# A length-48 first transform on the four quarters of the TensorE array, in a fused Fourier and mixture-of-experts kernel

## The chip, the cores and the metric

The kernel runs on one core of a Trainium2 chip. The metric is the device time of one execution in microseconds (us), as the median of the runs shown. A core has a matrix engine (TensorE, PE in the rows; PEld is its weight load), a vector engine (VectorE, DVE), an activation engine (ScalarE, ACT), a general engine (GpSimd, POOL) and a queue for transfers (SyncE, SP). Each works through its own instructions in order and waits for the others by semaphores.

## What is computed

```python
X = rfft(x, axis=1)                    # x: 8 batches, 3072 positions, 256 channels
Yr = Xr @ w_r - Xi @ w_i + b_r         # and Yi = Xr @ w_i + Xi @ w_r + b_i
Y = soft_threshold(Yr, 0.01) + 1j * soft_threshold(Yi, 0.01)
y = irfft(Y, n=3072, axis=1)           # 24576 tokens of 256 channels
logits = y @ phi                       # 32 slots of 8 experts
slot_out = experts(softmax(logits, 0).T @ y)      # relu(s @ w1[e]) @ w2[e]
z = softmax(logits, 1) @ slot_out
out = (silu(z @ w_gate) * (z @ w_val)) @ w_out
```

## The kernel before

The program has two parts. The first (`phase1`, up to about 584 us, then the experts up to 612 us) goes over the eight batches; the second (from 612 us, lines 1540 to 1590) is one long loop for the gated product and is not touched. `phase1` is a list of tasks, each with an engine and what it needs; a table of numbers, `ORDER`, written out in the file, gives the order in which all tasks of all engines are issued. Rings (`plan.ring`) say how many buffers each kind of tile has; a task that opens a buffer comes after the last user of the one that it replaces.

A batch goes through these stages:

- **Loads.** `load_x` (L571, on SP) brings 64 of the 256 channels of a batch: 96 partitions, each with 32 neighbouring positions of 64 channels. There are two such buffers (`xq`). Batch 0 has four own buffers (`load_first`, L557).
- **Stage A** (`stage_a`, matmul L586, transpose L591). The 3072 positions are 96 rows by 32. One matmul contracts the 96 rows with a table `fwd` of 128 columns (real and imaginary parts of two sets of 32 frequencies) for 32 x 16 = 512 columns of data, into one PSUM bank of the ring `ac`, which has two. VectorE turns the bank in 32 x 32 blocks into `chan`. There are 16 such pairs of matmul and transpose in a batch, four to a loaded tile. All of this is float32.
- **Stage C** (`stage_c`, L612) finishes the transform: for each of 24 columns `j` a matmul of `chan` (contraction over 128 rows) with the table `cm`, four to a bank of the same ring `ac`. ScalarE and VectorE take the bank apart into a rounded part and a rest (`xg`, L628 and L631) and a sum (`sf`, `sg`, L634 to L650).
- **Stage B** (`stage_b`, L700) multiplies by the weights `whl`, three fp32r matmuls of 512 columns at a time, into the ring `pb`; L752 to L771 apply bias and threshold; L797 projects on `phi` and 64 small transfers `yi` (L826) rearrange the result.
- **Logits, slots, combine** (L865 to L1241) form logits, the running softmax and the slot sums. Between them `narrow` (L1201 to L1246) converts weights through a buffer `cv`.

Several stages already use parts of the array. L797 and L1103 have weights of 32 columns and put four products into four groups of 32 output partitions; L1522 does it with two groups of 64. All of them contract over all the rows that they have from partition 0.

At the end of `phase1` the expert weights (16 transfers of 1 MB, L427 and L432, on POOL) go into buffers that stages A to C give up. `hold` (L1387) issues spare matmuls.

Of the kernel before, what the change touches and what calls it, by code (L numbers as in the profile page):

```python
# [10 lines left out]
F32 = mybir.dt.float32  # L11
# [12 lines left out]
R2 = 32  # L24
NCH = 24
# [7 lines left out]
def dft_tables():  # L33
# [7 lines left out]
    n1 = np.arange(R1)  # L41
    n2 = np.arange(R2)
    k2 = np.arange(R2)
    sign = np.where(k2 >= R2 // 2, -1.0, 1.0)
    alt1 = np.where(n1 % 2 == 0, 1.0, -1.0)
    alt2 = np.where(n2 % 2 == 0, 1.0, -1.0)
    k1 = np.array([[j, 23 + j] for j in range(NCH)])
    k1[0] = (0, 47)

    fwd = np.zeros((R1, 4, 32))  # L50
    mix = np.zeros((4, R2, NCH, 2, 2, R2))
    for j in range(NCH):
        for h in range(2):
            if j == 0 and h == 0:
                fwd[:, 0, 0] = 1.0
                fwd[:, 1, 0] = alt1
                for i in range(R2):
                    if i == 0:
                        mix[0, :, j, 0, h, 0] = 1.0
                        continue  # L60
                    src = 0 if i < 16 else 1
                    k = 96 * i if i < 16 else 48 + 96 * (i - 16)
                    a = 2 * np.pi * ((n2 * k) % n) / n
                    mix[src, :, j, 0, h, i] = np.cos(a)
                    mix[src, :, j, 1, h, i] = -np.sin(a)
                continue
            a = 2 * np.pi * ((n1 * k1[j, h]) % R1) / R1
            fwd[:, 2 * h, j] = np.cos(a)
            fwd[:, 2 * h + 1, j] = -np.sin(a)
            a = 2 * np.pi * ((n2[:, None] * (k1[j, h] + 96 * k2)[None, :]) % n) / n  # L70
            mix[2 * h, :, j, 0, h, :] = np.cos(a)
            mix[2 * h + 1, :, j, 0, h, :] = np.sin(a)
            mix[2 * h, :, j, 1, h, :] = -np.sin(a) * sign
            mix[2 * h + 1, :, j, 1, h, :] = np.cos(a) * sign
# [64 lines left out]

    small = np.concatenate(  # L140
        [
            pad(np.concatenate([np.zeros((R1, 8)), fwd.reshape(R1, 128)], 1), R1),
# [17 lines left out]
for _n, _w in (  # L160
# [11 lines left out]
FWD = 136  # L172
# [1523 lines left out]
```

## Time and profile before

| | |
|---|---|
| median of 3 runs | 1693.27 us (1691.08 to 1694.23) |
| the profiled execution, its own time | 1693.74 us |
| its span, first to last instruction | 1691.6 us |
| mean granted TensorE clock | 0.998 |
| PE busy | 1662.7 us, 98% |
| VectorE busy | 1296.0 us, 77% |
| ScalarE busy | 980.7 us, 58% |
| GpSimd busy | 312.5 us, 18% |

Busy time is the union of an engine's instructions. A line of a group gives the source line, the engine, the operation, output and inputs, shapes and count, then busy time, mean nanoseconds of one, the idle time of the engine before them and what ended it. A float32 matmul shows as two records of the same form, so a count of x4 is two matmuls; a fp32r one shows as one. The records of matmuls that follow each other overlap, so the mean of one record is longer than what it adds; the chain of waits shows what each adds.

### The profile page before, as it was taken

Reading aid. Unit: us, or ns where it says so; the run is one execution under the profiler, and the core shown is the slowest. Engines: PE = TensorE matmul, PEld = TensorE weight load, DVE = VectorE, ACT = ScalarE, POOL = GpSimd, SP = SyncE. Lnnn points to the kernel's source line nnn. Section 1 sums busy time; section 2 is a strip of 40 time slices with the busy share of each in tenths; the row PEclk is TensorE's granted clock in tenths of the full one; section 3 lists DMA queues with packets and bytes.
Section 4 is the critical chain, followed back from the end, with each engine's and each line's share of the span. In section 5 each row is a group of like instructions: output and inputs, shape, how many; then the busy total and the mean of one; then the engine's idle time right before and its main releaser. Section 6 shows DMA issues by size and latency. Waiting matters only on the chain.

```text
span 1691.6 us, 23302 instructions
## 1 busy us (share of the span) xinstructions
PE 1662.7 (98%) x8178; PEld 1284.8 (76%) x8178; DVE 1296.0 (77%) x2203; ACT 980.7 (58%) x1830; POOL 312.5 (18%) x360
## 2 busy tenths in 40 slices
PE   7999999999999889999999999999999999999998
PEld 4677776776777558888888888888888888888886
DVE  5788888888778458778777777777777777877776
ACT  2655664655657246666656655665666656655664
POOL 1234433334444521100200200200010110110000
PEclk9999999999999999999999999999999999999999
DMA  9465666766556981311311311311230131131111
GB/s 193 88 139 120 123 123 144 138 142 122 126 132 216 310 200 26 81 26 26 81 19 20 82 25 26 70 37 25 41 66 15 24 81 26 25 72 26 25 26 25
DMA packets 260036, 139.94 MB, mean 83 GB/s; under 512 B 210224, under 2 KB 243728, under 8 KB 259920
## 3 DMA queue, kind: packets, MB, share of 16 engines
q1 hardware_dynamic: 246592, 105.03, 31.0%
q0 software_dynamic: 12272, 33.17, 7.2%
q8 instruction: 65, 1.06, 0.3%
q10 hardware_dynamic: 1056, 0.26, 0.1%
q14 instruction: 51, 0.42, 0.1%
HBM read 72.74 MB, written 40.50 MB: 67 GB/s over the span
## 4 chain that ended last, share of the span: by engine, by line
PE 94%; DMA 3%; DVE 1%; POOL 1%; ACT 0%; issue 0%; SPq 0%; DVEq 0%; ACTq 0%
PE o L1572 47%; PE pb L700 11%; PE pg L1547 8%; PE pv L1548 8%; PE ac L586 7%; PE ac L612 5%; PE ch L797 1%; PE ch L865 1%; PE ch L1055 1%; DMA w1s<-in_moe_w_dram 1%; PE ch L1103 1%; DMA w2s<-in_moe_w_dram 1%; PE ch L925 1%; PE ch L1011 1%; PE po L1460 1%; DMA xq<-in_x_dram 0%
## 5 line engine op out<-in xcount | busy, mean ns | idle before, releaser
L1572 PE MATMUL o<-hh,wo 128*128 128x512 f32 x2304 | 722.5, 395 | 0.0
L1550 ACT ACTIVATE sg<-pg 128x512 f32<-128x512 f32 x576 | 344.6, 598 | 413.8 <-PE pg L1547 413.8
L1552 DVE TENSOR_TENSOR h<-sg,pv 128x512 f32<-128x512 f32 x576 | 393.2, 683 | 248.6 <-ACT sg L1550 245.3
L1572 PEld LDWEIGHTS o<-hh,wo 128*128 128x128 f32 x2304 | 434.2, 188 | 100.8
L1572 PE MATMUL o<-hl,wo 128*128 128x512 f32 x1152 | 453.8, 394 | 0.0
L1560 DVE TENSOR_TENSOR hl<-h,hh 128x512 fp32r<-128x512 f32 x576 | 396.7, 689 | 0.1
L1559 ACT ACTIVATE hh<-h 128x512 fp32r<-128x512 f32 x576 | 359.4, 624 | 0.3 <-DVE h L1552 0.2
L1572 PEld LDWEIGHTS o<-hl,wo 128*128 128x128 f32 x1152 | 216.1, 188 | 51.9
L1547 PE MATMUL pg<-cst,gstk 96*128 96x512 f32 x576 | 227.7, 395 | 0.0
L1548 PE MATMUL pv<-cst,gstk 96*128 96x512 f32 x576 | 226.1, 393 | 0.6 <-DVE gstk L1533 0.6
L700 PE MATMUL pb<-xg,whl 128*128 128x512 f32 x576 | 179.3, 441 | 0.0
L700 PEld LDWEIGHTS pb<-xg,whl 128*128 128x128 f32 x576 | 105.3, 189 | 46.5 <-issue 25.1
L1548 PEld LDWEIGHTS pv<-cst,gstk 96*128 96x128 f32 x576 | 109.7, 190 | 25.9 <-DVE gstk L1533 0.9
L1547 PEld LDWEIGHTS pg<-cst,gstk 96*128 96x128 f32 x576 | 108.1, 188 | 25.7 <-DVE gstk L1533 0.8
L771 POOL TENSOR_TENSOR yt<-r,yt 128x512 f32<-128x512 f32 x74 | 96.6, 1305 | 153.5 <-ACT yt L762 103.2
L591 DVE STREAM_TRANSPOSE chan<-ac 128x512 f32<-128x512 f32 x128 | 89.8, 708 | 34.1 <-PE ac L586 29.8
L1608 POOL TENSOR_TENSOR e<-e,rs 96x256 f32<-96x256 f32 x28 | 22.6, 834 | 498.8 <-DVE rs L1605 498.8
L586 PE MATMUL ac<-xq,fwd 96*128 96x512 f32 x224 | 110.3, 598 | 1.2 <-DVE chan L591 0.7
L612 PEld LDWEIGHTS ac<-cm,chan 128*128 128x128 f32 x768 | 101.0, 196 | 12.1 <-issue 4.5
L612 PE MATMUL ac<-cm,chan 128*128 128x128 f32 x768 | 105.3, 283 | 0.0
L700 PE MATMUL pb<-sg,whl 128*128 128x512 f32 x288 | 86.7, 425 | 0.0
L634 ACT ACTIVATE sf<-ac 128x256 f32<-128x256 f32 x96 | 36.5, 381 | 78.5 <-PE ac L612 74.4
(151 smaller groups left out, 1481.1 us busy)
## 6 DMA issues: line engine op xcount, KB each, us to landing
out_dram<-ob SPq DMA_DIRECT2D x190, 128.0 KB, 2.8
yi<-yt SPq DMA_DIRECT2D x368, 64.0 KB, 2.1
xq<-in_x_dram SPq DMA_DIRECT2D x28, 768.0 KB, 8.1
cst<-c_scr POOLq DMA_DIRECT2D x72, 128.0 KB, 3.1
w1s<-in_moe_w_dram POOLq DMA_DIRECT2D x8, 1024.0 KB, 9.0
w2s<-in_moe_w_dram POOLq DMA_DIRECT2D x8, 1024.0 KB, 10.9
x<-in_x_dram SPq DMA_DIRECT2D x4, 768.0 KB, 10.1
cv<-in_moe_w_gate_dram SPq DMA_DIRECT2D x6, 512.0 KB, 6.0
```

Source lines behind the costliest of these rows:

```text
L586: nc.tensor.matmul(out=pt, lhsT=fwd[:, 8 - 8 * dh:136 - 8 * dh], rhs=T[kq][:, :, d1:d1 + 16], start=True, stop=True)
L591: nc.vector.transpose(out=chan[:, 12 * dh:12 * dh + 16, d0:d0 + 16, :].rearrange("p j d i -> p d j i"), in_=T[ka].rearrange("p n d -> p d n"),
L612: nc.tensor.matmul(out=pt[:, :, q:q + 2, i // 2, :], lhsT=chan[:, 16 * dh + j // 2, :, j % 2], rhs=cm[:, j, :].rearrange("p (c h k) -> p c ...
L700: nc.tensor.matmul(out=pt, lhsT=w[:, dh, m, es], rhs=xx, start=m != 1 and dh == 0 and n == 0, stop=dh == 1 and n == 2, skip_group_check=True,)
L771: e.tensor_sub(out=part(), in0=quarters(T[kr]), in1=part())
L1547: nc.tensor.matmul(out=pg, lhsT=gstk[:, 0, f * 128:(f + 1) * 128], rhs=rhs, start=True, stop=True)
L1548: nc.tensor.matmul(out=pv, lhsT=gstk[:, 1, f * 128:(f + 1) * 128], rhs=rhs, start=True, stop=True)
L1550: nc.scalar.activation(out=sg, in_=pg, func=AF.Silu)
L1552: nc.vector.tensor_mul(out=h, in0=sg, in1=pv)
L1559: nc.scalar.activation(out=hh, in_=h, func=AF.Copy)
L1560: nc.vector.tensor_sub(out=hl, in0=h, in1=hh.bitcast(F32))
L1572: nc.tensor.matmul(out=po_t[0][k], lhsT=w[:, f % 4, k * 128:(k + 1) * 128], rhs=a, start=(f == 0 and m == 0), stop=(f == NF - 1 and m == 2 ...
```

## The change

Positions are now 48 rows by two halves by 32: position = 64 p + 32 h + n. A length-48 transform with the same 64 columns (32 frequencies, real and imaginary) is made of each half h, and stage C joins the halves. The table `fwd` has 72 columns rather than 136 and stands twice in its tile, from partition 0 and from partition 64. Stage C keeps its form and count; only the numbers in `cm` differ.

A loaded tile holds one half of the sequence: channels 0 to 63 of a 128-channel group on partitions 0 to 47 and channels 64 to 127 on partitions 64 to 111, brought by two transfers (`load_x`, `load_x2`). The ring `xq` has three buffers rather than two. For batches 1 to 7 one task issues four matmuls of 48 rows by 64 columns by 512, one for each quarter of the array, into both banks of `ac`; two transposes follow. For batch 0 one task issues two matmuls, on two diagonal quarters, into one bank, and the second half of its loads is issued by ScalarE. The order table is new; it also gives 16 small subtractions from VectorE to GpSimd and takes one back, and four more spare matmuls.

```diff
 ORDER = [
-    2, 1, 0, 3, 4, 5, 40, 30, 50, 312, 48, 49, 6, 8, 7, 9, 10, 12, 11, 13,
...
-            ("xq", 2), ("tt", 2), ("ac", 2), ("xg", 2), ("sf", 2), ("sg", 1), ("pb", 3), ("r", 1), ("yt", 2), ("yi", 4),
+            ("xq", 3), ("tt", 2), ("ac", 2), ("xg", 2), ("sf", 2), ("sg", 1), ("pb", 3), ("r", 1), ("yt", 2), ("yi", 4),
...
-        fwd = apool.tile([R1, FWD], F32, name="fwd")
+        fwd = apool.tile([64 + R0, FWD], F32, name="fwd")
...
+        def half_x(k, r):
+            _, b, dh, c = k
+            d0 = 128 * dh + 64 * r
+            nc.sync.dma_start(
+                out=T[k][64 * r:64 * r + R0],
+                in_=x[b, :, d0:d0 + 64].rearrange("(p h n) d -> h p n d", h=2, n=R2)[c],
+            )
...
+        def stage_a0(dq, dd, rank):
...
+                for r in range(2):
+                    rows = slice(64 * r, 64 * r + R0)
+                    nc.tensor.matmul(
+                        out=pt[64 * r:64 * r + 64], lhsT=fwd[rows, 8 - 8 * dh:72 - 8 * dh],
+                        rhs=T["x0", dq][rows, :, 16 * dd:16 * dd + 16], start=True, stop=True, skip_group_check=True,
+                    )
...
+        def stage_a(b, dh, dd, rank):
+            kq = [("xq", b, dh, c) for c in range(2)]
...
+            def mm():
+                pt = [bank(k, [128, R2, 16], "ac") for k in ka]
+                for r, c in ((0, 0), (1, 1), (0, 1), (1, 0)):
+                    rows = slice(64 * r, 64 * r + R0)
+                    nc.tensor.matmul(
+                        out=pt[r][64 * c:64 * c + 64], lhsT=fwd[rows, 8 - 8 * dh:72 - 8 * dh],
+                        rhs=T[kq[c]][rows, :, d1:d1 + 16], start=True, stop=True, skip_group_check=True,
+                    )
...
+            for r in range(2):
+                add("DVE", turn(r), r=[ka[r]], w=[(*kt, ps[r])])
```

The new lines carry new numbers: L643 is the matmul of the quarters, L651 its transpose, L615 and L621 those of batch 0, L589 the load, L765 is the old L700, L677 the old L612, L862 the old L797, L891 the old L826, L1266 the old L1201, L1306 the old L1241, L1076 the old L1011, L1040 the old L975.

TensorE's order in the first stage A after batch 0 (batch 1, channels 0 to 127), before:

```order
L586 MATMUL ac<-xq,fwd 128x512
L700 MATMUL pb<-sg,whl 128x512 x3
L700 MATMUL pb<-xg,whl 128x512 x6
L586 MATMUL ac<-xq,fwd 128x512 x2
L700 MATMUL pb<-xg,whl 128x512 x3
L586 MATMUL ac<-xq,fwd 128x512 x2
L700 MATMUL pb<-xg,whl 128x512 x3
L586 MATMUL ac<-xq,fwd 128x512
L700 MATMUL pb<-xg,whl 128x512 x3
L586 MATMUL ac<-xq,fwd 128x512 x2
```

and the same place now:

```order
L643 MATMUL ac<-xq,fwd 64x512 x4
L765 MATMUL pb<-sg,whl 128x512 x6
L643 MATMUL ac<-xq,fwd 64x512 x4
L765 MATMUL pb<-xg,whl 128x512 x6
L643 MATMUL ac<-xq,fwd 64x512 x4
L765 MATMUL pb<-xg,whl 128x512 x6
L643 MATMUL ac<-xq,fwd 64x512 x4
L862 MATMUL ch<-yt,phis 32x256 x4
```

Eight matmuls of the old kind have become four groups of four; between two groups there are mostly six matmuls of stage B where three stood between two pairs.

TensorE's order in batch 5, from the end of channels 0 to 127 to the start of channels 128 to 255, before (from the last two matmuls on the second of the batch's four tiles to the first on the third):

```order
L586 MATMUL ac<-xq,fwd 128x512
L700 MATMUL pb<-xg,whl 128x512 x3
L586 MATMUL ac<-xq,fwd 128x512
L700 MATMUL pb<-xg,whl 128x512 x3
L1011 MATMUL ch<-td,csm 128x512
L612 MATMUL ac<-cm,chan 128x2x2x32 x8
L1011 MATMUL ch<-td,csm 128x512
L700 MATMUL pb<-sg,whl 128x512 x3
L1055 MATMUL ch<-vpad,csm 128x192 x4
L1061 MATMUL ch<-vt,csm 32x16 x2
L700 MATMUL pb<-sg,whl 128x512 x3
L586 MATMUL ac<-xq,fwd 128x512
```

and now:

```order
L643 MATMUL ac<-xq,fwd 64x512 x4
L765 MATMUL pb<-xg,whl 128x512 x3
L1076 MATMUL ch<-td,csm 128x512
L677 MATMUL ac<-cm,chan 128x2x2x32 x8
L765 MATMUL pb<-sg,whl 128x512 x3
L1076 MATMUL ch<-td,csm 128x512
L862 MATMUL ch<-yt,phis 32x256 x8
L677 MATMUL ac<-cm,chan 128x2x2x32 x4
L765 MATMUL pb<-sg,whl 128x512 x6
L765 MATMUL pb<-xg,whl 128x512 x3
L765 MATMUL pb<-sg,whl 128x512 x3
L643 MATMUL ac<-xq,fwd 64x512 x4
```

The work between the last group on one pair of tiles and the first group on the next pair is what stands in this list; the second tile of the next pair takes a buffer of the first pair.

The loads of batch 5 on the SP queue, before (the first three of its four tiles):

```order
L571 DMA xq<-in_x_dram 96x32x64
L826 DMA yi<-yt 32x2x256 x16
L571 DMA xq<-in_x_dram 96x32x64
L826 DMA yi<-yt 32x2x256 x16
L1241 DMA w_scr_60<-cv 128x512
L1201 DMA cv<-in_moe_w_out_dram 128x2x512
L571 DMA xq<-in_x_dram 96x32x64
```

and now (both halves of the third tile, then those of the fourth):

```order
L589 DMA xq<-in_x_dram 48x32x64 x2
L1306 DMA w_scr_60<-cv 128x512
L589 DMA xq<-in_x_dram 48x32x64
L1266 DMA cv<-in_moe_w_val_dram 128x1024
L589 DMA xq<-in_x_dram 48x32x64
L891 DMA yi<-yt 32x2x256 x16
```

One transfer of 96 partitions has become two of 48, and a conversion load (L1266) stands between the two halves of the tile that waits for its buffer.

## Rows read from the trace of the kernel before

**Rows 1.** The page: busy time, its 40 slices, and the chain by engine and line.

```profile
PE 1662.7 (98%) x8178; PEld 1284.8 (76%) x8178; DVE 1296.0 (77%) x2203; ACT 980.7 (58%) x1830; POOL 312.5 (18%) x360
...
PEclk9999999999999999999999999999999999999999
...
PE o L1572 47%; PE pb L700 11%; PE pg L1547 8%; PE pv L1548 8%; PE ac L586 7%; PE ac L612 5%; PE ch L797 1%; PE ch L865 1%; PE ch L1055 1%; DMA w1s<-in_moe_w_dram 1%; PE ch L1103 1%; DMA w2s<-in_moe_w_dram 1%; PE ch L925 1%; PE ch L1011 1%; PE po L1460 1%; DMA xq<-in_x_dram 0%
```

**Rows 2.** Windows: stretch, length, busy us (instructions) by engine, clock, DMA share, GB/s.

```profile
0.00:26.00 26.00, 17.87 (x34) 6.36 (x35) 11.65 (x20) 1.28 (x1) 0.70 (x6) 1.00 1.18 195
...
50.00:550.00 500.00, 497.45 (x2904) 359.28 (x2903) 421.28 (x750) 294.97 (x587) 189.50 (x178) 1.00 0.63 136
...
584.00:612.00 28.00, 23.67 (x233) 10.21 (x232) 4.18 (x37) 5.60 (x10) 9.81 (x15) 0.94 1.09 332
```

**Rows 3.** Groups of instructions: the first transform and the work moved between engines.

```profile
L586 PE MATMUL ac<-xq,fwd 96*128 96x512 f32 x224 | 110.3, 598 | 1.2 <-DVE chan L591 0.7 <-DMA xq<-in_x_dram 0.4
L771 POOL TENSOR_TENSOR yt<-r,yt 128x512 f32<-128x512 f32 x74 | 96.6, 1305 | 153.5 <-ACT yt L762 103.2 <-ACT r L762 29.3 <-DMA xq<-in_x_dram 10.7
L650 POOL TENSOR_TENSOR sg<-sf,sg 128x256 fp32r<-128x256 f32 x74 | 55.6, 755 | 99.2 <-ACT sg L646 92.3 <-DMA yi<-yt 4.7 <-issue 1.1
L771 DVE TENSOR_TENSOR yt<-r,yt 128x512 f32<-128x512 f32 x22 | 15.0, 683 | 5.0 <-ACT r L762 2.6 <-ACT yt L762 2.2
L650 DVE TENSOR_TENSOR sg<-sf,sg 128x256 fp32r<-128x256 f32 x22 | 9.4, 429 | 1.8 <-ACT sg L646 1.2 <-issue 0.5
```

**Rows 4.** Chain of waits from 105 us: start, us it adds, what.

```profile
108.12 0.93 PE ac L612 x8
...
113.57 1.72 PE ac L586 x4
115.29 0.70 PE pb L700 x3
115.99 1.00 PE ch L797 x16
...
119.16 0.86 PE ch L1011 x2
```

**Rows 5.** Timeline of VectorE from 14.9 us: batch 0's transposes back to back.

```profile
16.92 1.57 DVE L591 STREAM_TRANSPOSE chan<-ac 128x512 f32<-128x512 f32 x2 [0.36 <-PE ac L586]
18.86 1.57 DVE L591 STREAM_TRANSPOSE chan<-ac 128x512 f32<-128x512 f32 x2 [0.36 <-PE ac L586]
...
24.67 0.72 DVE L591 STREAM_TRANSPOSE chan<-ac 128x512 f32<-128x512 f32 x1 [0.36 <-PE ac L586]
```

**Rows 6.** Line L571 on the SP queue: nanoseconds of an issue, then us to landing.

```profile
L571 SPq DMA_DIRECT2D xq<-in_x_dram x28: 569/604/3834, 22.3 to 482.5; - x28
...
DMA to landing us min/median/max: 6.7/8.1/11.6
```

**Rows 7.** DMA issues: transfers, KB each, median us from issue to landing.

```profile
cv<-in_moe_w_val_dram SPq DMA_DIRECT2D x6, 512.0 KB, 4.1
```

**Rows 8.** Timeline from 0 us: first instructions of TensorE, and ScalarE's first.

```profile
8.13 17.36 PE L586 MATMUL ac<-x,fwd 96*128 96x512 f32 x30 [8.13 <-DMA fwd<-in_csmall_dram]
...
26.69 0.38 ACT L634 ACTIVATE sf<-ac 128x256 f32<-128x256 f32 x1 [24.66 <-PE ac L612]
```

**Rows 9.** Waits of TensorE on transfers: who, for what, us in total, times, longest.

```profile
PE po L1460 <- DMA w2s<-in_moe_w_dram: 3.2, 1, 3.2
...
PE ch L1103 <- DMA w2s<-in_moe_w_dram: 1.1, 1, 1.1
```

More of the change, by code (lines that the diff above doesn't have):

```diff
@@ L24 @@
 R2 = 32
+R0 = 48
 NCH = 24
@@ L41, in dft_tables @@
     n1 = np.arange(R1)
+    m1 = np.arange(R0)
+    m2 = np.arange(2 * R2)
     n2 = np.arange(R2)
@@ L45, in dft_tables, with put_mix @@
     alt1 = np.where(n1 % 2 == 0, 1.0, -1.0)
+    alt0 = np.where(m1 % 2 == 0, 1.0, -1.0)
     alt2 = np.where(n2 % 2 == 0, 1.0, -1.0)
[L47 to L51, printed above, removed]
-    for j in range(NCH):
+    k1 = np.array([[j, 48 + j] for j in range(NCH)])
+    k1[0] = (0, 24)
+    fwd = np.zeros((R0, 2, 32))
+    mix = np.zeros((2, 2, R2, NCH, 2, 2, R2))
+    def put_mix(part, j, c, h, i, v):
+        mix[:, part, :, j, c, h, i] = v.reshape((2, R2) + v.shape[1:])
@@ L53, in dft_tables @@
+    every = slice(None)
+    for j in range(NCH):
+        if j == 0:
+            fwd[:, 0, 0] = 1.0
+            fwd[:, 1, 0] = alt0
+        else:
+            a = 2 * np.pi * ((m1 * j) % R0) / R0
+            fwd[:, 0, j] = np.cos(a)
+            fwd[:, 1, j] = -np.sin(a)
         for h in range(2):
             if j == 0 and h == 0:
[L55 to L61, printed above, removed]
+                put_mix(0, j, 0, h, 0, np.ones(2 * R2))
+                for i in range(1, R2):
@@ L69, in dft_tables @@
[L69 to L74, printed above, removed]
+            a = 2 * np.pi * ((m2[:, None] * (k1[j, h] + 96 * k2)[None, :]) % n) / n
+            if j == 0:
+                put_mix(1, j, 0, h, every, np.cos(a))
+                put_mix(1, j, 1, h, every, -np.sin(a) * sign)
+                continue
@@ L76, in dft_tables @@
+            put_mix(0, j, 0, h, every, np.cos(a))
+            put_mix(1, j, 0, h, every, np.sin(a))
+            put_mix(0, j, 1, h, every, -np.sin(a) * sign)
+            put_mix(1, j, 1, h, every, np.cos(a) * sign)
     kn = 2 * np.pi * (np.outer(k2, n2) % R2) / R2
@@ L131, in dft_tables @@
     last[0:32, 0] = alt2
+    last[64:96, 0] = alt2
     fold = np.tile(np.eye(32), (4, 4))
@@ L138, in pad @@
         return z
+    first = np.zeros((128, FWD))
+    for r in range(2):
+        first[64 * r:64 * r + R0, 8:] = fwd.reshape(R0, 64)
     small = np.concatenate(
         [
-            pad(np.concatenate([np.zeros((R1, 8)), fwd.reshape(R1, 128)], 1), R1),
+            first,
             pad(gf.reshape(R1, 128), R1),
@@ L171 @@
     _o += _w
-FWD = 136
+FWD = 72
 SMW = _o
@@ L508, in load_f @@
         def load_f():
-            nc.sync.dma_start(out=fwd, in_=csmall[0:R1, 0:FWD])
+            nc.sync.dma_start(out=fwd, in_=csmall[0:64 + R0, 0:FWD])
         def mix_w():
@@ L551, in phase1, with load_first @@
         add("DVE", setup_small, w=["small", "vpad", "M"])
-        def load_first(dq):
+        def load_first(dq, r):
             def go():
-                T["x0", dq] = t = early.tile([R1, R2, 64], F32, name=f"x0{dq}")
-                nc.sync.dma_start(
-                    out=t, in_=x[0, :, dq * 64:(dq + 1) * 64].rearrange("(p n) d -> p n d", n=R2)
+                if ("x0", dq) not in T:
+                    T["x0", dq] = early.tile([64 + R0, R2, 64], F32, name=f"x0{dq}")
+                (nc.sync, nc.scalar)[r].dma_start(
+                    out=T["x0", dq][64 * r:64 * r + R0],
+                    in_=x[0, :, 64 * dq:64 * dq + 64].rearrange("(p h n) d -> h p n d", h=2, n=R2)[r],
                 )
@@ L566, in free_early, with load_x, load_x2, go @@
             ypool = open_pool("ypool")
[L568 removed]
+        def half_x(k, r):
[5 more added lines that the diff above has]
+            )
+        def load_x(k):
             def go():
[L570 to L578 removed]
+                sb(xpool, k, [64 + R0, R2, 64], "xq", 3)
+                half_x(k, 0)
+            return go
+        def load_x2(k):
+            def go():
+                half_x(k, 1)
+            return go
+        def stage_a0(dq, dd, rank):
             dh, d0 = dq // 2, (dq % 2) * 64 + dd * 16
[L580 to L582 removed]
+            ka = ("ac", "a", 0, 4 * dq + dd)
             def mm():
                 pt = bank(ka, [128, R2, 16], "ac")
[L586 to L588 removed]
+                for r in range(2):
[4 more added lines that the diff above has]
+                    )
             def turn():
@@ L594, in turn, with go @@
                 )
-            add("PE", mm, r=["f", kq, kt], w=[ka], new=[("ac", ka)] + ([("tt", kt)] if p % 8 == 0 else []))
-            add("DVE", turn, r=[ka], w=[(*kt, p)])
+            kt = ("tt", 0, dh)
+            add(
+                "PE", mm, r=["f", kt] + [("x0", dq, r) for r in range(2)], w=[ka], new=[("ac", ka)] + ([("tt", kt)] if d0 == 0 else []),
+            )
+            add("DVE", turn, r=[ka], w=[(*kt, 4 * dq + dd)])
+        def stage_a(b, dh, dd, rank):
+            kq = [("xq", b, dh, c) for c in range(2)]
+            kt = ("tt", b, dh)
+            ps = [8 * dh + 4 * r + dd for r in range(2)]
+            ka = [("ac", "a", b, p) for p in ps]
+            d1 = dd * 16
+            def mm():
[5 more added lines that the diff above has]
+                        rhs=T[kq[c]][rows, :, d1:d1 + 16], start=True, stop=True, skip_group_check=True,
+                    )
+            def turn(r):
+                def go():
+                    d0 = 64 * r + d1
+                    nc.vector.transpose(
+                        out=chan[:, 12 * dh:12 * dh + 16, d0:d0 + 16, :].rearrange("p j d i -> p d j i"),
+                        in_=T[ka[r]].rearrange("p n d -> p d n"),
+                    )
+                return go
+            add(
+                "PE", mm, r=["f", kt] + [(*k, r) for k in kq for r in range(2)], w=ka, new=[("ac", k) for k in ka] + ([("tt", kt)] if dd == 0 else []),
+            )
+            for r in range(2):
+                add("DVE", turn(r), r=[ka[r]], w=[(*kt, ps[r])])
         def stage_c(b, g, hb, dh, rank):
@@ L1298, in phase1 @@
             for dq in range(4 * (b == 0)):
-                add("SP", load_first(dq), w=[("x0", dq)])
-            for dq in range(4):
-                if b == 0 and dq == 3:
+                for r, q in enumerate(("SP", "ACT")):
+                    add(q, load_first(dq, r), w=[("x0", dq, r)])
+                if dq == 3:
                     constants(0)
-                if b:
-                    add("SP", load_x(b, dq), w=[("xq", b, dq)], new=("xq", ("xq", b, dq)))
-                for p in range(4 * dq, 4 * dq + 4):
-                    stage_a(b, p, a0 + p * da)
+                for dd in range(4):
+                    stage_a0(dq, dd, a0 + (4 * dq + dd) * da)
+            for dh in range(2 * (b > 0)):
+                for c in range(2):
+                    k = ("xq", b, dh, c)
+                    t = a0 - 1.0 + (8 * dh + 4 * c) * da
+                    add("SP", load_x(k), w=[(*k, 0)], new=("xq", k))
+                    add("SP", load_x2(k), w=[(*k, 1)])
+                for dd in range(4):
+                    stage_a(b, dh, dd, a0 + (8 * dh + 2 * dd) * da)
             if b == 0:
```

21 lines of the change are left out of this document (3 added, 18 removed), and 240 rows, old and new, of the table ORDER.

## The prediction

> **What bounds the kernel now.** I read the page first: TensorE is busy for 98% of the span, the chain that ends last is nearly all PE, and the clock is at its upper level throughout [rows 1]. So a microsecond taken from TensorE counts, as long as nothing else becomes late. Half of the chain belongs to the second part of the program, which the change leaves alone; the first transform, L586, has 7% of it [rows 1], about 115 us. I then took the windows to see the stage around the change. From 50 to 550 us TensorE is busy for 497.45 of 500 us and VectorE for 421.28, which is 84% [rows 2]. VectorE is the engine next in line, and it holds the banks of the ring `ac` that stage A fills. Last I read the chain for what an instruction really adds: four records of L586, which are two float32 matmuls, add 1.72 us, so 0.86 us each [rows 4]; the 598 ns of the group line is longer than one record's share because records overlap [rows 3].
>
> **Removed and added on TensorE.** Batches 1 to 7 have 7 x 16 = 112 matmuls of L586 (the x224 of the group are two records each [rows 3]), 112 x 0.86 = 96.3 us. In their place stand 7 x 8 = 56 groups of four, each with the same 512 columns. If the quarters of the array work side by side, a group streams in the time of one matmul, 0.86 us; one after another the four take 3.44 us.
>
> The trace shows half of this. L797 puts eight matmuls of 256 columns (x16 records) on four groups of columns and they add 1.00 us [rows 4]. Four side by side, twice, would stream in 2 x 0.43 = 0.86 us by the rate of L586, and one after another in 3.44 us. So column groups do run side by side, and a change of form into and out of such a group costs some 0.14 us. Whether two groups of rows also run side by side no row shows: everything here contracts from partition 0. The bounds of a group are thus 0.86 us (all side by side and the switch free) and 1.72 + 0.14 = 1.86 us (only columns side by side); 3.44 us is excluded by L797. I take 1.00 us, the price of L797, since it is the nearest row in every respect but the rows. That saves 56 x (1.72 - 1.00) = **40.3 us**; the bounds are 48.2 us saved and 7.8 us lost.
>
> [...]
>
> **The hand-over to VectorE.** A group now takes both banks of `ac`, and the next user needs them turned. In batch 0 the transposes run at TensorE's heels: two come every 1.93 us [rows 5], which is one matmul, 0.86 us, one transpose, 0.72 us, and 0.35 us of passing the bank to and fro. After a group two transposes follow, so the next group can start 2 x 0.72 + 0.35 = 1.79 us after the end of this one. In the new order the usual filling is six matmuls of L765; three of L700 add 0.70 us [rows 4], so six are 1.40 us and 0.39 us is missing. I counted the 42 places between groups: 11 have just these six (4.3 us missing in all), eight others have 1.1 to 1.75 us of work (about 2.2 us), the rest enough. That adds **6.5 us** of waiting. Below, it is 0 if the hand-over is quicker; above, it grows with VectorE's load (a rival).
>
> **The loads.** Before, a tile took the buffer of the last but one. Now a pair of tiles is used by all four groups of a half, and the second tile of the next pair needs a buffer of this pair. So each batch has one crossing in its middle at which the load starts only when the fourth group ends. It needs two issues of 0.60 us and, for the same 768 KB, 8.1 us to landing (6.7 to 11.6) [rows 6], with the hand-over 9.5 us. The work between, by the order and the prices of [rows 4] (in batch 5: 18 matmuls of L765 at 0.233, two of L1076 at 0.86, 12 of L677 at 0.235, L862 1.00), is 9.7 us there, 9.2 and 9.0 us in batches 4 and 6, and 11 to 18 us in the other four. In batch 5 a conversion load stands between the two halves on the queue (4.1 us [rows 7]), in batch 6 four stores. Short by 0 in all three if the fastest landing holds and the transfers overlap; by 0.3, 3.9 and 4.6 us if nothing overlaps. I take **5 us**, the middle of 0 and 9. The second crossing, between batches, has 24 us of work and more and is covered; without this cover it would cost as the first does.
>
> **What is hidden.** Sixteen subtractions go to GpSimd and one comes back; VectorE loses 10 x 0.43 + 6 x 0.68 - 0.69 = 7.7 us and GpSimd gains 10 x 0.755 + 6 x 1.305 - 1.31 = 14 us [rows 3], on an engine busy for 189.50 of 500 us [rows 2]. The 28 more load issues are 17 us spread over SP, where only the crossings above wait for them. ScalarE's four load issues at the start come before its first work at 26.69 us [rows 8]. The four spare matmuls fill waits. Batch 0 keeps its pace: TensorE starts when `fwd` and the first data land at 8.13 us and its 15 matmuls take 17.36 us [rows 8]; a pair on diagonal quarters is one matmul's time, so 0. Weight loads at the end follow the last stage A, which now has some 84 us of TensorE work behind it by the order and the same prices, against 77; TensorE waits 3.2 and 1.1 us for them [rows 9]. If a later buffer made them late they would cost up to that again; I take 0.
>
> **The sum.** 1693.7 us of the profiled execution - 40.3 + 6.5 + 5 = 1664.9 us. The median of the runs is 0.5 us lower, so **1665 us** on either.
>
> **The rivals.**
> - **Row groups do not run side by side (slower).** Then a group is 1.86 us, 56 x 0.14 = 7.8 us more than before; the hand-overs and loads still cost 6.5 + 5; and in batch 0 each pair takes 1.72 us in place of the 0.97 us at which the hand-over paced it, 16 x 0.75 = 12 us with nothing to cover it. That is 1693.7 + 31 = 1725 us. It decides from a group price of 1.52 us, where the saving is eaten by the 11.5 us of waits. For it: no row shows two row groups. Against it: four column groups, each with data of its own, cost nothing in L797.
> - **Row groups run side by side, but not into one bank.** The groups of batches 1 to 7 give each row half its own bank; the pairs of batch 0 write one. Then only those 12 us are lost: 1677 us. [...]
> - **VectorE becomes the bound.** It keeps 421.3 - 7.7 = 413.6 us of work in what were 500 us. At my sum it would be at 88%; if its in-order queue cannot be kept fuller than the 84% of now [rows 2], the stretch lasts 413.6 / 0.8426 = 491 us and only 9 us are gained: 1685 us. For it: both banks now hang on two transposes. Against it: TensorE waited for a transpose only 0.7 us on the matmul rows of L586 [rows 3].
> - **The time freed is lost to the loads.** If every crossing is short by 4.6 us, seven cost 32 us in place of 5: 1692 us, no change. The matmuls would be faster and the kernel not. Against it: four crossings have 11 us and more.
>
> **How the numbers follow.** My forecast has 0.62, row groups one after another 0.09, one bank 0.09, VectorE 0.14, loads 0.06. The forecast's own range is the sum with its bounds: 48.2 saved and 0 waits would be 1645 us, which needs all three at their best, so I go to 1650; at the other end 33 saved and 17 of waits is 1678 us. The range of 8 in 10 goes on to take in the one-bank and VectorE cases: 1650 to 1687. It leaves out row groups one after another, the loads at their worst and the tails. A measurement here can tell about 0.2%, 3.4 us. Faster: 0.62 + 0.09 + nearly all of VectorE's 0.14 = 0.84; same: the loads' case, 0.05; slower: 0.11.
>
> **What would show it.** Right: eight records of L643 add about 1.00 us in the chain; TensorE's idle time before L643 is some 6 us by transposes and some 5 us by the loads; batch 0 ends by 26 us as now; VectorE is at 88% of the middle stretch; the second part keeps its 1080 us. Wrong: L643 at 1.8 us (row groups), batch 0 ending 12 us later (one bank), idle before L643 and L677 by VectorE of 20 us and more, or idle by the loads of 4 us in every batch.

## The result, and the profile after

The changed kernel took 1709.01 us (median of 4 runs, 1708.22 to 1716.01) beside 1693.75 us (4 runs, 1691.08 to 1695.28) for the kernel before: a ratio of 1.0103 (95% interval 1.0087 to 1.0118), 15 us slower. The prediction was 1665 us and faster, with a range of 1650 to 1687 us. The sign was wrong and the miss is 44 us. The profiled execution took 1708.45 us.

Page of the changed kernel: DMA issues (count, KB each, median us to landing).

```profile
xq<-in_x_dram SPq DMA_DIRECT2D x56, 384.0 KB, 8.5
```

Windows of the changed kernel, columns as in [rows 2].

```profile
50.00:550.00 500.00, 483.58 (x3092) 324.11 (x3090) 405.35 (x727) 289.36 (x580) 193.86 (x184) 0.98 0.78 128
...
100.00:150.00 50.00, 46.32 (x272) 30.64 (x271) 43.01 (x77) 28.04 (x56) 22.98 (x21) 0.93 0.77 120
```

Where 50 to 550 us had TensorE busy for 497.45 us at full clock and a DMA share of 0.63 [rows 2], it is now busy for 483.58 us at 0.98, and the DMA engines are busier (0.78) while they move less (128 GB/s against 136). VectorE has fallen to 405.35 us, 81%: it is not the new bound. A load of 384 KB now takes 8.5 us to land, longer than 768 KB took before [rows 6].

Groups of the changed kernel, shapes apart, 0 to 605 us: busy, mean ns | idle before, and what ended it.

```profile
L643 PE MATMUL ac<-xq,fwd 48*64 48x512 f32 x448 | 75.3, 628 | 5.5 <-DMA xq<-in_x_dram 4.1 <-DVE chan L651 0.7 <-PE ch L862 0.5
...
L643 PEld LDWEIGHTS ac<-xq,fwd 48*64 48x64 f32 x448 | 15.6, 133 | 34.9 <-issue 14.6 <-DVE chan L651 7.6 <-DVE xg L696 2.7
```

Chain of waits of the changed kernel, 105 to 155 us: start, us it adds, what.

```profile
109.99 9.09 DMA xq<-in_x_dram
119.07 0.14 issue
119.21 1.98 PE ac L643 x6
121.19 2.76 PE pb L765 x6
123.95 1.02 PE ac L643 x8
124.97 1.60 PE pb L765 x6
...
131.68 6.13 DMA xq<-in_x_dram
...
143.57 7.69 DMA xq<-in_x_dram
```

Two things stand here. Eight records of L643 do add 1.02 us: the quarters run side by side, row groups too. And the loads of `xq`, 0% of the chain before [rows 1], now stand in it again and again: three landings of 6.1 to 9.1 us in 50 us. From 50 to 550 us they are 13.5% of the chain, where they were 1.6% before. The wait costs twice. TensorE stands idle for 2.96 us before the group at 119.21 us; then six records take 1.98 us and L765 takes 2.76 us, where eight records and the same L765 take 1.02 and 1.60 us a little later. The granted clock was 0.50 from 118 to 121 us and 1.00 again from 124 us.

One sign misleads. The prediction looked for the cost of the loads in TensorE's idle time before L643, some 5 us, and the groups above show 4.1 us there. The experiments show that the loads cost far more than this row.

The start is late as well. Batch 0's loads land after 15.1 and 16.0 us (SyncE's and ScalarE's queue), and TensorE starts at 9.29 us and stops twice.

Timeline of the changed kernel, 0 to 40 us: TensorE's work on batch 0.

```profile
9.29 11.22 PE L615 MATMUL ac<-x,fwd 48*64 48x512 f32 x34 [9.29 <-DMA fwd<-in_csmall_dram]
...
21.85 3.81 PE L615 MATMUL ac<-x,fwd 48*64 48x512 f32 x14 [1.33 <-DMA x<-in_x_dram]
...
27.46 4.49 PE L615 MATMUL ac<-x,fwd 48*64 48x512 f32 x12 [1.80 <-DMA x<-in_x_dram]
```

### The profile page after: what moved, and what is told of

Same layout as the page of the kernel before. It is cut to its first block, busy times and chain, and to the rows that moved or that the text cites. A ratio compares the mean times of both kernels' runs of the same rounds, so it can differ in the third digit from the quotient of the medians.

```text
span 1706.7 us, 23803 instructions
## 1 busy us (share of the span) xinstructions
PE 1658.6 (97%) x8442; PEld 1254.3 (73%) x8442; DVE 1288.0 (75%) x2188; ACT 979.9 (57%) x1830; POOL 324.3 (19%) x375
## 4 chain that ended last, share of the span: by engine, by line
PE 83%; DMA 9%; DVE 2%; SPq 2%; ACT 2%; issue 1%; POOL 1%; ACTq 0%; DVEq 0%; POOLq 0%
PE o L1643 47%; PE pg L1618 8%; PE pv L1619 8%; PE pb L765 8%; DMA xq<-in_x_dram 4%; PE ac L677 3%; PE ac L643 3%; DMA yi<-yt 2%; DMA x<-in_x_dram 2%; SPq L891 1%; PE ch L1168 1%; PE ch L930 1%; PE ch L862 1%; PE ch L1120 1%; PE ch L1076 0%
## 5 line engine op out<-in xcount | busy, mean ns | idle before, releaser
L765 PE MATMUL pb<-xg,whl 128*128 128x512 f32 x576 | 164.6, 420 | 8.8 <-ACT yt L817 8.5
L765 PEld LDWEIGHTS pb<-xg,whl 128*128 128x128 f32 x576 | 103.5, 191 | 61.5 <-issue 20.4
L836 POOL TENSOR_TENSOR yt<-r,yt 128x512 f32<-128x512 f32 x80 | 104.4, 1306 | 174.9 <-ACT yt L827 119.4
L1679 POOL TENSOR_TENSOR e<-e,rs 96x256 f32<-96x256 f32 x28 | 22.6, 834 | 498.4 <-DVE rs L1676 498.4
L677 PEld LDWEIGHTS ac<-cm,chan 128*128 128x128 f32 x768 | 100.0, 196 | 14.5 <-issue 4.6
L677 PE MATMUL ac<-cm,chan 128*128 128x128 f32 x768 | 104.3, 284 | 0.5 <-DVE chan L651 0.3
L651 DVE STREAM_TRANSPOSE chan<-ac 128x512 f32<-128x512 f32 x112 | 74.0, 694 | 31.2 <-PE ac L643 30.8
L715 POOL TENSOR_TENSOR sg<-sf,sg 128x256 fp32r<-128x256 f32 x84 | 61.9, 742 | 142.6 <-ACT sg L711 127.5
L765 PE MATMUL pb<-sg,whl 128*128 128x512 f32 x288 | 84.6, 420 | 1.0 <-DVE yt L820 0.9
L693 ACT ACTIVATE xg<-ac 128x512 fp32r<-128x512 f32 x96 | 56.5, 593 | 49.5 <-PE ac L677 31.1
```

The source lines that it names most:

```text
L651: nc.vector.transpose(out=chan[:, 12 * dh:12 * dh + 16, d0:d0 + 16, :].rearrange("p j d i -> p d j i"), in_=T[ka[r]].rearrange("p n d -> p ...
L677: nc.tensor.matmul(out=pt[:, :, q:q + 2, i // 2, :], lhsT=chan[:, 16 * dh + j // 2, :, j % 2], rhs=cm[:, j, :].rearrange("p (c h k) -> p c ...
L715: e.tensor_sub(out=sview(1), in0=T[ks], in1=sview(0).bitcast(F32))
L765: nc.tensor.matmul(out=pt, lhsT=w[:, dh, m, es], rhs=xx, start=m != 1 and dh == 0 and n == 0, stop=dh == 1 and n == 2, skip_group_check=True,)
L836: e.tensor_sub(out=part(), in0=quarters(T[kr]), in1=part())
```

## The experiments

The first theory was that a transfer into 48 partitions lands at half the rate; the rivals were the hand-overs to VectorE, the new order, and the greater number of transfers.

**1. Loads alone (m1_loads).** A small kernel that does only such loads.

> Loads alone, one after the other, each awaited before the next, six of a kind; nothing else of the computation is there and the output is not the reference's. Theory (a load is slow when its partitions lie in 0-47 or in 64-111 only): the whole tile (96 partitions, 768 KB) lands in 5 to 8 us, and the half tile on 48 partitions (384 KB) in about the same time, 80 to 110% of it; the same 384 KB spread over 96 partitions (16 positions each) in 50 to 70% of the whole tile's time; 48 partitions from 48 to 95 in between; two halves issued together take 1.6 times the whole tile or more. Rival 1 (a fixed cost for each transfer): every 384 KB load lands alike, wherever its partitions are. Rival 2 (every other block of 32 positions is skipped in the source): 48 partitions with a source without gaps land in 50 to 70% of the whole tile's time, those with gaps do not.

Page of this run: DMA issues, median us to landing.

```profile
full<-in_x_dram SPq DMA_DIRECT2D x6, 768.0 KB, 6.3
...
low<-in_x_dram SPq DMA_DIRECT2D x6, 384.0 KB, 5.0
high<-in_x_dram SPq DMA_DIRECT2D x6, 384.0 KB, 5.1
mid<-in_x_dram SPq DMA_DIRECT2D x6, 384.0 KB, 3.9
dense<-in_x_dram SPq DMA_DIRECT2D x6, 384.0 KB, 5.3
half<-in_x_dram SPq DMA_DIRECT2D x6, 384.0 KB, 3.6
```

384 KB landed in 5.0 us on partitions 0 to 47, in 5.1 us on 64 to 111, in 3.9 us on 48 to 95 and in 3.6 us over 96. A fixed cost per transfer is out, since equal sizes differ. So are the gaps in the source: 48 partitions read without gaps took 5.3 us. The partitions count, as the theory says, but less than it says: 5.0 of 6.3 us is 79%, where 80 to 110% were expected, and two halves issued together took 1.25 times the whole tile (8.1 against 6.5 us), not 1.6 times or more.

**2. The loads taken away, or spread (a_few, a_wide).**

```diff
-                out=T[k][64 * r:64 * r + R0],
-                in_=x[b, :, d0:d0 + 64].rearrange("(p h n) d -> h p n d", h=2, n=R2)[c],
+                out=T[k][0:R1, 16 * r:16 * r + 16],
+                in_=x[b, :, d0:d0 + 64].rearrange("(p n) d -> p n d", n=R2)[:, 16 * c:16 * c + 16],
```

(a_wide; a_few keeps the form and loads 2 of the 32 positions.)

> The changed kernel, with the loads of batches 1 to 7 reduced to 2 of the 32 positions once the ring is full (the rest of the tile keeps old data, so the transform there is of wrong input). Theory (the loss is in the landing of these loads): the time falls from 1709 to 1655-1672 us, since the 40 us of cheaper matmuls come through and only the start and the hand-overs stay. Rival (the loss is in the hand-overs to VectorE or in the new order of the work, not in the loads): 1698-1710 us.

> The changed kernel, with each load of batches 1 to 7 of the same size and packets (384 KB in packets of 256 bytes, two to a tile, on the same queue) but over 96 partitions by 16 positions and not 48 by 32 (the transform then works on rows that do not belong to it). Theory (the partitions make the load slow): loads land in 4 to 7 us and the time is 1658-1676 us. Rival (it is the number or the size of the transfers): landing stays at 8 to 9 us and the time at 1700-1712 us. In between: both have a part.

They took 1686.07 us (ratio to before 0.9955, 0.9940 to 0.9970) and 1686.66 us (0.9963, 0.9950 to 0.9976). Spread over 96 partitions the loads landed in 5.7 us and cost no more than next to no loads at all: they are then hidden. So the loads of batches 1 to 7 account for 22 us of the changed kernel, and their number does not. But both runs missed the 1655 to 1676 us expected: another 20 us were missing that are not in these loads.

**3. The kernel before with split loads (b_split).**

```diff
-                nc.sync.dma_start(
-                    out=t, in_=x[b, :, dq * 64:(dq + 1) * 64].rearrange("(p n) d -> p n d", n=R2)
-                )
+                v = x[b, :, dq * 64:(dq + 1) * 64].rearrange("(p h n) d -> h p n d", h=2, n=R2)
+                nc.sync.dma_start(out=t[:R1 // 2], in_=v[0])
+                nc.sync.dma_start(out=t[R1 // 2:], in_=v[1])
```

> The kernel before, with each 768 KB load of batches 1 to 7 issued as two of 48 partitions (0-47 and 48-95, even and odd blocks of 32 positions, so rows are permuted). No matmul changes. Theory (48-partition loads alone cost the time): 1705-1740 us, with waits for the loads on TensorE that the kernel before has not. Rival (the loads are hidden, and the loss needs the new order or the quarters): 1690-1698 us.

1706.62 us (1.0072, 1.0055 to 1.0089): the form of the loads slows the kernel before by 13 us, without quarters and without the new order. Landing was 7.7 us for each half.

**4. Quarters alone (m2_quarters).** A small kernel of matmuls only.

> TensorE alone, 16 repetitions of each short sequence; nothing else of the computation is there and the output is not the reference's. Three 128x512 matmuls of the large stage take 0.70 us in the traces, a full-width transform matmul 0.86 us more, two of them 1.72 us more. Theory (going into the quarters and out of them costs time, because weights are not loaded ahead under a quarter-tile matmul): three such matmuls and a group of four quarters take 0.70 + 1.02 + 0.3 to 0.4 = 2.0 to 2.15 us a repetition, and two groups of four in a row add about 1.0 us for the second; a run of groups of four without anything between takes 1.0 us each. Rival (the quarters cost 1.02 us wherever they stand, and the rest of the missing time is in waits for other engines): 1.70 to 1.78 us a repetition.

Timeline of TensorE in this run: L35 is the 128x512 matmul, L38 the full-width transform, L42 the quarters. The repetition time is the distance of two rows of L35; L54 is the same matmul, sixteen in a row.

```profile
46.80 3.79 PE L54 MATMUL pb<-xg,w 128*128 128x512 f32 x16
50.42 0.85 PE L35 MATMUL pb<-xg,w 128*128 128x512 f32 x3
...
53.13 1.25 PE L35 MATMUL pb<-xg,w 128*128 128x512 f32 x3
54.22 1.02 PE L38 MATMUL ac<-xq,fwd 96*128 96x512 f32 x2
54.68 1.25 PE L35 MATMUL pb<-xg,w 128*128 128x512 f32 x3
...
77.19 1.26 PE L35 MATMUL pb<-xg,w 128*128 128x512 f32 x3
...
79.61 1.27 PE L35 MATMUL pb<-xg,w 128*128 128x512 f32 x3
...
115.67 0.96 PE L35 MATMUL pb<-xg,w 128*128 128x512 f32 x3
116.56 1.09 PE L42 MATMUL ac<-xq,fwd 48*64 48x512 f32 x8
117.58 0.96 PE L35 MATMUL pb<-xg,w 128*128 128x512 f32 x3
...
279.03 14.82 PE L42 MATMUL ac<-xq,fwd 48*64 48x512 f32 x136
293.78 14.00 PE L38 MATMUL ac<-xq,fwd 96*128 96x512 f32 x32
```

A repetition takes 1.55 us with one full-width transform matmul, 2.42 with two and 1.91 with a group of quarters. Sixteen in a row take 50.42 - 46.80 = 3.62 us, so three of L35 are 0.68 us and a group in its place costs 1.23 us. Seventeen groups in a row take 293.78 - 279.03 = 14.75 us, 0.87 us each. Going in and out of the quarters thus costs 0.36 us a time, whatever is done between: a single quarter-tile matmul between two groups of L35 also took a repetition of 1.89 us. The expected 2.0 to 2.15 us was too much, the rival's 1.70 to 1.78 too little. TensorE's weight loads point to why: under the quarters the next weights are not loaded ahead, as these rows of the same run show.

```profile
54.65 0.19 PEld L35 LDWEIGHTS pb<-xg,w 128*128 128x128 f32 x1 [0.24 <-issue]
...
116.56 0.21 PEld L42 LDWEIGHTS ac<-xq,fwd 48*64 48x64 f32 x8 [0.36 <-issue]
117.58 0.53 PEld L35 LDWEIGHTS pb<-xg,w 128*128 128x128 f32 x3 [0.81 <-issue]
```

After a full-width transform the load of L35's first weights starts at 54.65, 0.59 us before the transform ends (54.22 + 1.02); after the quarters it starts at 117.58, 0.07 us before they end (116.56 + 1.09). What else the 0.36 us for the way in and out together are made of, this run does not show.

**5. Batch 0 as before (a_first), and the second halves on ScalarE's queue (a_act, a_both).** a_first puts the 96-row loads and full-width matmuls back for batch 0, with a second table `fw0`:

```diff
+        fw0 = apool.tile([R1, 136], F32, name="fw0")
...
+                    T["x0", dq] = early.tile([R1, R2, 64], F32, name=f"x0{dq}")
+                    nc.sync.dma_start(
+                        out=T["x0", dq],
+                        in_=x[0, :, 64 * dq:64 * dq + 64].rearrange("(p n) d -> p n d", n=R2),
+                    )
...
+                nc.tensor.matmul(
+                    out=pt, lhsT=fw0[:, 8 - 8 * dh:136 - 8 * dh],
+                    rhs=T["x0", dq][:, :, 16 * dd:16 * dd + 16], start=True, stop=True,
+                )
```

a_act changes two places, and a_both has both edits:

```diff
-            nc.sync.dma_start(
+            (nc.sync, nc.scalar)[r].dma_start(
...
-                    add("SP", load_x2(k), w=[(*k, 1)])
+                    add("ACT", load_x2(k), w=[(*k, 1)])
```

> The changed kernel with batch 0 as it was before: four loads of 96 partitions and 768 KB on one queue, 16 full-width matmuls on a second table; all else as changed. Theory (the start of the changed kernel is late because its 48-partition loads land late): the first transform ends at 28 to 31 us and not at 36, and the time falls by 5 to 8 us, to 1701-1704 us. Rival (the late start is made up by the slack of the first batch): 1707-1711 us.

> The changed kernel with the second half of each tile of batches 1 to 7 loaded from ScalarE's queue, the first from SyncE's as it was. In the loads-alone run two halves on one queue took 8.1 us together and on two queues 6.7 us, as long as one whole tile (6.5 us). Theory (the halves on different sides of partition 64 only stand in each other's way because they follow one another on a queue): 1688-1698 us. Rival (ScalarE now waits in order for ring places and loses more than that): 1705-1725 us.

> The two edits before together. If they add up: 1681-1692 us, less than the kernel before. If the start is covered by other slack: as the run with ScalarE's queue alone.

a_act took 1782.69 us (1.0515, 1.0489 to 1.0542) and a_both 1737.50 us (1.0260, 1.0245 to 1.0276). The rival had the direction right, but a_act lies far beyond its 1705 to 1725 us, and a_both is neither at the 1681 to 1692 us of two edits that add up nor at a_act's time. In a_act the loads from ScalarE's queue landed in 6.0 us, yet TensorE waited 37.0 us for the tiles in eight waits. The second halves were issued late: in the median 17.3 us after the first, in the changed kernel 4.9 us. That ScalarE's own in-order work held them back is argued from this, not shown by a run.

a_first took 1676.38 us (0.9901, 0.9886 to 0.9916): 33 us less than the changed kernel, where 5 to 8 were expected. The last matmul of the first transform started at 29.6 us, as expected, but the loads of batches 1 to 7, whose form is unchanged, now landed in 6.2 us. The theory of the partitions alone fell here. The trace's packet records say the same: from 50 to 500 us a 256-byte packet took 40.4 ns on average in the changed kernel and 24.4 ns here.

What a_first had changed besides was a place in memory. Tiles lie one behind another in a partition, and the table `fwd` stands ahead of the `xq` tiles in that row. The row is laid from the upper end of the partition downwards, so what is added ahead of a tile lowers the address at which it begins. With the changed kernel's 72 columns (288 bytes) the tiles begin 32 bytes past a multiple of 256 bytes, in the kernel before (136 columns) as well, and batch 0's tiles too. The 544 bytes of `fw0` (512 and 32) moved the `xq` tiles to a multiple of 512.

**6. The place of the tile (m3_offsets, a_align, a_align2, b_align).**

```diff
-        fwd = apool.tile([64 + R0, FWD], F32, name="fwd")
+        fwd = apool.tile([64 + R0, FWD + 8], F32, name="fwd")[:, 0:FWD]
...
-        phis = chp.tile([128, 2, 32], F32, name="phis")
+        phis = chp.tile([128, 120], F32, name="phis")[:, 0:64].rearrange("p (k s) -> p k s", k=2)
```

(a_align has the first edit, a_align2 both, b_align the like in the kernel before. Batch 0's tiles lie behind `phis` in a row that is laid upwards, so the 224 bytes more raise them.)

> Loads alone again, six of a kind, each awaited: the whole tile (96 partitions, 768 KB), the half tile at partitions 0-47 and at 64-111, 384 KB over 96 partitions, and two half tiles on one queue; into a tile that begins 0, 32, 64 and 128 bytes past a multiple of 256 bytes in its partition. In the first loads-alone run, and in the kernels before and after, it began 32 bytes past one; in the run with batch 0 as before it began at one. [...] If 64 and 128 bytes are as slow as 32, the multiple is 256; if they are as fast as 0, it is 64. Rival (only the partitions count): half tile about 5 us at every offset.

> The changed kernel with 32 bytes more behind the transform's table, so that the tiles of batches 1 to 7 begin at a multiple of 512 bytes and not 32 bytes past one; nothing else. The packets of these loads took 40 ns each in the changed kernel and 24 ns in the run with batch 0 as before, where the longer table had moved the tiles to such a multiple. Theory (the place of the tile in its partition made the loads slow): loads land in 5.8 to 6.5 us at the median and not 8.5, and the time is 1679-1689 us. Rival (the late batch 0 made the rest late, and what it changed is what counts): 1704-1711 us.

> As the run before, and the tiles of batch 0 (and what lies behind them: the inverse transform's tiles) begin at a multiple of 512 bytes as well, by 224 bytes more in a table ahead of them. Theory: the loads of batch 0 land sooner too, the first transform ends at 29 to 33 us and not at 36, and the time is 1672-1684 us. Rival: no change from the run before.

> The kernel before with the same two shifts (its tiles also begin 32 bytes past a multiple of 256 bytes). [...] Rival (any tile placed so costs time): 1670-1685 us.

One number in the first of these is mistaken: in m1_loads the tile began 160 bytes past a multiple of 256, not 32.

m3_offsets, by line: L39 whole tile, L44 partitions 0 to 47 and L54 384 KB over 96 partitions at offset 0; L65, L70 and L80 the same at 32; L96 partitions 0 to 47 at 64 (min/median/max to landing under each).

```profile
L39 SPq DMA_DIRECT2D big<-in_x_dram x6: 563/564/713, 0.7 to 30.7; - x6
DMA to landing us min/median/max: 5.2/5.3/5.6
L44 SPq DMA_DIRECT2D big<-in_x_dram x6: 311/312/352, 36.4 to 60.8; - x6
DMA to landing us min/median/max: 4.3/4.5/5.0
...
L54 SPq DMA_DIRECT2D big<-in_x_dram x6: 312/313/313, 68.2 to 87.9; - x6
DMA to landing us min/median/max: 3.2/3.3/3.5
...
L65 SPq DMA_DIRECT2D big<-in_x_dram x6: 563/568/570, 123.6 to 159.9; - x6
DMA to landing us min/median/max: 6.6/6.7/6.7
L70 SPq DMA_DIRECT2D big<-in_x_dram x6: 311/312/320, 166.9 to 203.1; - x6
DMA to landing us min/median/max: 6.1/6.8/7.3
...
L80 SPq DMA_DIRECT2D big<-in_x_dram x6: 312/313/313, 213.1 to 235.2; - x6
DMA to landing us min/median/max: 3.8/3.8/3.9
...
L96 SPq DMA_DIRECT2D big<-in_x_dram x6: 311/312/317, 326.0 to 357.0; - x6
DMA to landing us min/median/max: 5.3/5.9/6.5
```

At offset 32 a half tile takes as long as a whole one, 6.8 and 6.7 us; at 0 they take 4.5 and 5.3. The author's estimate for the half tile, 5.0 us at 32 bytes as in m1_loads and 3.6 to 4.2 us at 0, had the direction right and the sizes wrong; the rival, the same time at every offset, falls. At 64 and at 128 bytes the half tile takes 5.9 us, so a multiple of 64 or 128 is not enough; 256 is, since b_align's tiles begin 256 bytes past a multiple of 512 and their packets are the fastest seen (table below). The same 384 KB over 96 partitions took 3.3 us at 0 and 3.8 at 32. Both things count, then, and each makes the other worse: the partitions cost 1.2 us (4.5 against 3.3) at a good place and 3.0 us (6.8 against 3.8) at a bad one. The whole tile gained 1.4 us, where the author's estimate was less than 0.8.

In the kernels: a_align 1686.80 us (0.9952, 0.9937 to 0.9968), a_align2 1673.70 us (0.9875, 0.9861 to 0.9890), b_align 1688.53 us (0.9963, 0.9952 to 0.9975), with loads that land 1.5 us sooner than before; the author's estimate was 1688 to 1695 us and 0 to 1 us sooner. DMA issues of b_align, then of a_align2.

```profile
xq<-in_x_dram SPq DMA_DIRECT2D x28, 768.0 KB, 6.6
```

```profile
xq<-in_x_dram SPq DMA_DIRECT2D x56, 384.0 KB, 6.0
x<-in_x_dram ACTq DMA_DIRECT2D x4, 384.0 KB, 11.2
x<-in_x_dram SPq DMA_DIRECT2D x4, 384.0 KB, 11.0
```

Thirty-two unused bytes take 22 us off the changed kernel, as much as taking the loads away did, and the second shift another 13 us: the last matmul of batch 0's transform starts at 28.7 us and not at 38.4 as in a_align. That shift also moves the inverse transform's tiles. Their part was not tried alone, but it is small if the parts add: a_best (experiment 7) differs from a_first by this shift alone, with batch 0's loads over 96 partitions in both, and is faster by 2.3 us, or by 4.2 us when each is set against the kernel before beside it. The first shift moves the table `cm` as well, which is not told apart here. Mean times of a 256-byte packet from 50 to 500 us show both causes:

| | tile 32 bytes off | tile at a multiple of 256 |
|---|---|---|
| 96 partitions, 768 KB | 27.9 ns (before) | 18.3 ns (b_align) |
| 48 partitions, 384 KB | 40.4 ns (after) | 24.0 ns (a_align2) |

In a_wide, 96 partitions in pieces of 384 KB and still 32 bytes off, the mean is 24.3 ns: there, too, taking away one of the two causes was enough.

Why packets into 48 partitions take longer than packets into 96 (40.4 against 27.9 ns, 24.0 against 18.3 ns), and packets into a tile 32 bytes off longer than into one at a multiple of 256, no run here shows.

**7. What the quarters save in their place (a_single), and the best version (a_best).**

```diff
-                for r, c in ((0, 0), (1, 1), (0, 1), (1, 0)):
-                    rows = slice(64 * r, 64 * r + R0)
+                for r in range(2):
                     nc.tensor.matmul(
-                        out=pt[r][64 * c:64 * c + 64], lhsT=fwd[rows, 8 - 8 * dh:72 - 8 * dh],
-                        rhs=T[kq[c]][rows, :, d1:d1 + 16], start=True, stop=True, skip_group_check=True,
+                        out=pt[r], lhsT=fwd[0:R1, 8 - 8 * dh:136 - 8 * dh],
+                        rhs=T[kq[r]][0:R1, :, d1:d1 + 16], start=True, stop=True, skip_group_check=True,
```

> The changed kernel with all its tiles at multiples of 256 bytes and the same order of work, but each group of four quarters of batches 1 to 7 replaced by two full-width matmuls over 96 rows, as in the kernel before (they transform rows that do not belong together). The difference to the run with all tiles so placed and quarters (1673.7 us) is what the quarters save where they stand. Theory (a group costs 0.86 us and 0.36 us for going in and out, 1.22 us alone and some 1.4 us in its place, against 1.72 us): 56 groups times 0.32 to 0.51 us, so 18 to 29 us slower, 1692-1703 us. By the price of the prediction (1.00 us): 40 us slower, 1710-1716 us. Rival (the saving is lost to other engines, so that the form of the transform hardly counts): 1674-1685 us.

> All tiles placed at multiples of 512 bytes, quarters in batches 1 to 7, and batch 0 as before: 768 KB loads over 96 partitions and full-width matmuls. With all tiles so placed the first transform ended at 29 us with 48-partition loads, and at 28 us in the kernel before with its tiles shifted. If batch 0's loads still cost: 1668-1672 us. If nothing is left there: 1672-1676 us.

a_single took 1700.46 us (1.0032, 1.0019 to 1.0044): 26.8 us more than a_align2, so a group saves 26.8 / 56 = 0.48 us where it stands. m2_quarters gives 2.42 - 1.91 = 0.51 us. The saving is not lost on other engines; it was smaller than predicted. a_best took 1674.13 us (0.9873, 0.9858 to 0.9888), the same as a_align2: nothing is left in batch 0.

a_align2 beats both kernels: by 1.25% (interval 1.10 to 1.39%) the kernel before, and b_align by 15 us.

## Why the prediction was wrong, step by step

The runs give the sum again: 1693.7 us before; the quarters -26.8 (a_align2 less a_single); the new order with half-tile loads and all else +11.9 (a_single less b_align); the place of the tiles +35.3 in the changed kernel (1709.0 less 1673.7), of which the kernel before already paid 6.2 (1694.8 less 1688.5). 1693.7 - 26.8 + 11.9 + 29.1 = 1707.9 us, against 1709.0 measured. Every term is a difference between these runs, so the sum closes by itself and proves nothing; what it gives is the sizes. Of the 44 us of the miss, 13.5 are the quarters and 29.1 the place of the tiles.

- **What bounds the kernel** was right, and VectorE did not become the bound (81%).
- **Quarters at 1.00 us: right mechanism, wrong size.** The predicted 40.3 us were 26.8. The chain still shows 1.02 us for a group, but the price of going in and out lies partly in the group that follows. I took L797's 1.00 us from its own row in the chain, and the price of the way out stands in the row behind it. The trace of the kernel before had it: one L586 matmul right after L797 adds 1.06 us there (chain below) in place of 0.86, and 1.00 + 0.20 = 1.20 us would have been close. The term measures 1.23 us, and 0.48 to 0.51 us saved, not 0.72. No run shows the 33 us saved at the slow end of the forecast's own range; a_single less a_align2 shows 26.8 us.
- **Hand-overs at 6.5 us: not seen.** L643 waits for `chan` for 7.6 us on its weight loads and 0.7 us on its matmuls. But L586 already waited 7.2 us (last row below) and 0.7 us [rows 3], so these rows show no added wait of that size.
- **The loads at 5 us: the step that failed.** It took 8.1 us of [rows 6] "for the same 768 KB" in two issues. A row of 96 partitions cannot stand for one of 48: the same bytes took 8.5 us for each half, and 40 ns a packet against 28. By a_wide the loads of batches 1 to 7 cost 22 us and not 5. Only 4.1 us of it is L643 waiting for a tile (groups above). Set against a_align2, with the tiles at a good place, TensorE stands idle for 41.7 us before the second part in place of 26.1, and by the trace's clock records it runs at a granted clock of 0.50 for 31 us of that stretch in place of 10 (7 in the kernel before). The rest of the way from the loads to the time no row shows. The rival "the time freed is lost to the loads" had the right place, but it too was priced by those 8.1 us, and it ended at no change. With tiles at a good place 11.9 us are left for hand-overs, loads and order together, where the prediction had 6.5 + 5 = 11.5. That is luck as far as the runs show: before the second part TensorE stands idle for 22.6 us in a_single and 19.6 us in b_align, so only 3 of the 11.9 us are idle time, and in a_align2 the matmuls of L643 wait at most 0.1 us for a transpose or a load. What the 11.9 us are made of stays open.
- **"Batch 0 keeps its pace": failed for the same reason.** Its matmuls kept it; its loads did not. The last matmul started at 35.7 us, where the kernel before has 29.3, and shifting the tiles brought it to 28.7. The term was put at 0; by a_align2 less a_align it was some 13 us.
- **The weight loads at the end stayed hidden:** from the last matmuls of the batches to the end the span is 1107.9 us before and 1102.7 us after. The other terms that were called hidden no run shows alone, and one wait is new: L765 waits 5.3 us for ScalarE's `yt` in a_align2, and the kernel before has no such wait.
- **One bank for two row groups: no cost.** Batch 0's pairs write one bank, and their transposes still come two in 1.90 us (below) as in [rows 5].

Timeline of VectorE in the changed kernel, batch 0; then two views of the kernel before: its chain at 186.50 us, and the weight loads of L586 as a group from 0 to 605 us.

```profile
16.74 1.57 DVE L621 STREAM_TRANSPOSE chan<-ac 128x512 f32<-128x512 f32 x2 [0.48 <-PE ac L615]
18.64 1.58 DVE L621 STREAM_TRANSPOSE chan<-ac 128x512 f32<-128x512 f32 x2 [0.33 <-PE ac L615]
```

```profile
186.50 1.00 PE ch L797 x16
187.50 1.06 PE ac L586 x2
```

```profile
L586 PEld LDWEIGHTS ac<-xq,fwd 96*128 96x128 f32 x224 | 41.1, 189 | 29.3 <-issue 14.7 <-DVE chan L591 7.2 <-DVE sf L637 0.8
```

## What to carry to other kernels

A transfer has a shape at its far end: the same 384 KB landed in 3.3 us over 96 partitions and in 4.5 us on 48 (m3_offsets, offset 0). When a change alters which partitions a load fills, or the length of anything that lies ahead of its tile, price the load anew, and look at where the tile begins: the place of the tiles was worth 35 us in the changed kernel, and the quarters 27 us. The packed matmuls had a price for going in and out, 0.36 us a time in m2_quarters; read such a price from the start of the group before to the start of the group after, not from the group's own row.

## What was not expected of the hardware

- A 256-byte packet into a tile 32 bytes off a multiple of 256 took 27.9 ns against 18.3 ns with 96 partitions, and 40.4 against 24.0 ns with 48. The kernel before paid for this too: 6 us of its 1694.
- Two half tiles together, at 160 bytes past such a multiple, took 8.1 us from one queue and 6.7 us from two, the whole tile 6.5 us (VectorE's waits in m1_loads, six of each: 48.4, 40.1 and 38.7 us). One half alone took 5.2 us by the same waits, so the halves are filled in part at the same time, and more so from two queues.
- One quarter-tile matmul between full-width ones costs as much time as four (a repetition of 1.89 against 1.91 us).
